# An adaLN transformer block on one core: the rows of w_mod dealt to the partitions in neighbouring fives, the conditioning vector loaded in that form, and the order of all instructions replaced

## The chip, the cores and the metric

The kernel runs on one core of a Trainium2 chip. The time is device microseconds of one execution, lower is better; a time given for a kernel is the median of its runs. One further execution is recorded by the hardware profiler, and all rows of the profile come from that one.

## The reference

```
mod = (silu(c) @ w_mod).reshape(1, 6, 1, 640)      # c: 1 x 640, w_mod: 640 x 3840
sa, ca, ga, sb, cb, gb = the six rows of mod
h = layernorm(x) * (1 + ca) + sa                    # x: 1 x 2048 x 640, bf16
q, k, v = split(h @ wqkv)                           # 32 heads of 20
p = softmax(where(0 <= i - j < 256, q k^T / sqrt(20), -1e9))
x = x + ga * ((p v) @ wo)
h = layernorm(x) * (1 + cb) + sb
x = x + gb * ((sigmoid(h @ w_gate) * (h @ w_up)) @ w_down)    # 640 -> 1536 -> 640
```

Only c and w_mod are touched in their layout. Whatever the order, out[f] = sum over the 640 rows d of silu(c)[d] · w_mod[d, f], so the rows may be dealt to the 128 partitions in any way as long as c is dealt in the same way.

## The kernel before, in words

The 2,048 rows are worked in chunks of 256. For a chunk, x is normalised (ln_stats on DVE and POOL), transposed to hT (columns on partitions, five tiles of 128), modulated with 1 + ca and sa, and projected with wqkv. The products q and k are laid out per head as QT and KT, by TensorE transpositions through PSUM in the first chunks (matmuls M from ident and stg) and later by DMA transpositions. The scores of four heads at a time are written to the PSUM tile S (L693), ACT takes their exp into E (L1019), POOL or DVE cuts out the window (L1044), TensorE multiplies E with V (bursts of matmuls M from E and V), DVE transposes the sums (L1088) and normalises into On, and SP stores On to a scratch array doc in HBM and loads it back as oT, transposed. Then come the output projection with wo (L1149 adds it to x), the second layer norm, and the feed-forward with the weights wg, wu and wd (sigmoid on ACT L1194, product on DVE L1196, result added at L1215). The score sets are interleaved with all other matmuls. For every chunk but the first there are, for each half of the heads, four main sets and one edge's set, which takes the blocks at both ends of the window; its score matmuls are 128x64.

At the start, silu of c is made in small steps and spread to a tile silubc; the modulation sums are matmuls of silubc with w_mod. w_mod comes in three parts of 1,280 columns, loaded into memory that later holds wd, wu and hh, so the profile calls them wd, wu and hh from in_w_mod_dram. wqkv comes in slices of columns (four of 320, then one of 640), all through SP's DMA queue in the order in which SP issues them. The gate ga is brought to HBM as `gate`, loaded to all partitions as gbc, and multiplied into wo on DVE (L1238), five times 128x640. Until real work is there, TensorE runs matmuls on zeros (L672, L682).

What sets the order is a table of numbers. `build()` records every operation in program order; the n-th recorded operation takes the n-th entry of PRIO. The entry modulo 5 names the engine (pe, act, dve, pool, sp), and the operations are issued on each engine in the order of their entries. The same walk hands out the buffers of each pool. `emit()` then writes the semaphore waits which the data and the buffers need, and makes POOL wait for DVE operations that hold the shared port ahead of it in the table.

```
        o.prio = PRIO[self.seq] if PRIO else prio
        for o in sorted(self.ops, key=lambda x: x.prio):
            e = ENGS[o.prio % 5]
```

c is loaded by ACT's queue in five rows of 128 numbers into a corner of the buffer of oT (c_row), transposed by one matmul with ident into PSUM (tile psc, 128x5) and halved by DVE into c_col, from which tanh and silu follow. Partition p so holds the numbers p, 128 + p, 256 + p, 384 + p and 512 + p of c, and the same five rows of w_mod.

Of the kernel before, what the change touches and what calls it, by code (L numbers as in the profile page):

```python
# [8 lines left out]
ALU = mybir.AluOpType  # L9
# [8 lines left out]
NDT = D // 128  # L18
# [343 lines left out]
def c_pe(n):  # L362
# [148 lines left out]
def build(nc, A_x, A_wqkv, A_wo, B_x, B_w_gate, B_w_up, B_w_down, c, w_mod, out, S=2048):  # L511
    NCH = S // CH
    P = Prog(nc)
    A = P.op
# [3 lines left out]
    def sb(name, shape, dtype=BF16):  # L518
        return nc.alloc_sbuf_tensor(name, shape, dtype)
# [9 lines left out]
    ident = sb("ident", [128, 128])  # L529
# [761 lines left out]
```

## Time and profile before

| | |
|---|---|
| median of 3 runs | 323.55 us (323.23 to 323.64) |
| profiled execution, its own time | 324.34 us |
| span of the profiled execution | 322.6 us |
| granted TensorE clock, mean | 1.000 |
| TensorE matmuls | 316.8 us busy, 4,877 |
| TensorE weight loads | 223.2 us, 4,877 |
| VectorE (DVE) | 207.1 us, 420 |
| ScalarE (ACT) | 218.0 us, 327 |
| GpSimd (POOL) | 177.0 us, 268 |
| HBM read, written | 21.30 MB, 5.25 MB |

The profile gives times from the span's start; "[0.80 <-DMA wqkv<-in_A_wqkv_dram]" behind a row is the idle time of that engine ahead of the row and what ended it. SPq and ACTq are the issues of DMAs on SP and ACT, not the transfers. A row with "x10" holds ten instructions of one shape one after the other, with the time from the start of the first to the end of the last.

### The profile page before, as it was taken

How to read it: one execution, taken by the hardware profiler on the slowest of the kernel's cores; microseconds unless marked ns; L12 is line 12 of the kernel's file. 1: busy time of each engine (PE TensorE's matmuls, PEld its weight loads, DVE VectorE, ACT ScalarE, POOL GpSimd, SP SyncE). 2: the span in 40 equal slices, each digit the busy share in tenths (PEclk: the TensorE clock that was granted, in tenths of full speed). 3: DMA queues.
4: the chain of work that ended last, by engine and by line, in shares of the span. 5: the costliest groups of instructions: out<-in, count | busy, mean ns of one | idle time of the engine just before them, and what ended most of it. 6: DMA issues, size and time to landing. Idle time of an engine off the chain costs nothing.

```text
span 322.6 us, 11622 instructions
## 1 busy us (share of the span) xinstructions
PE 316.8 (98%) x4877; PEld 223.2 (69%) x4877; DVE 207.1 (64%) x420; ACT 218.0 (68%) x327; POOL 177.0 (55%) x268
## 2 busy tenths in 40 slices
PE   8899999999999999999999999999999999999996
PEld 3565545556876577767766667876887788887885
DVE  5688997886689658683756565637572765464232
ACT  2689888799887979688878686877767563110120
POOL 4237985978566675856566555666547366002000
PEclk9999999999999999999999999999999999999999
DMA  7979999799992753465024572530222031305101
GB/s 229 364 246 394 233 214 177 146 171 207 274 156 48 118 93 87 99 95 144 9 63 93 94 111 69 71 93 13 68 65 67 2 83 34 90 3 63 42 22 41
DMA packets 71182, 37.85 MB, mean 117 GB/s; under 512 B 45274, under 2 KB 69338, under 8 KB 71130
## 3 DMA queue, kind: packets, MB, share of 16 engines
q1 hardware_dynamic: 70112, 35.96, 50.2%
q10 hardware_dynamic: 1018, 1.15, 1.1%
q8 instruction: 38, 0.62, 0.8%
q14 instruction: 14, 0.11, 0.1%
HBM read 21.30 MB, written 5.25 MB: 82 GB/s over the span
## 4 chain that ended last, share of the span: by engine, by line
PE 92%; SPq 3%; DMA 2%; issue 1%; ACT 1%; DVE 0%; ACTq 0%
PE M L692 76%; PE S L693 8%; PE M L693 7%; SPq L588 3%; DMA wqkv<-in_A_wqkv_dram 2%; ACT E L1019 1%; DVE hh L1196 0%; ACT sig L1194 0%; DVE x L1215 0%; ACTq L335 0%
## 5 line engine op out<-in xcount | busy, mean ns | idle before, releaser
L1019 ACT ACTIVATE E<-S 128x512 bf16<-128x512 f32 (+2 forms) x184 | 150.4, 878 | 38.1 <-PE S L693 34.9
L1044 POOL TENSOR_SCALAR_AFFINE_SELECT E<-E 128x512 bf16<-128x512 bf16 (+1 forms) x176 | 139.3, 819 | 58.1 <-ACT E L1019 18.8
L692 PE MATMUL M<-wqkv,hT 128*128 128x480 bf16 (+1 forms) x340 | 73.0, 355 | 1.6 <-DMA wqkv<-in_A_wqkv_dram 1.6
L692 PE MATMUL M<-h2T,wu 128*128 128x256 bf16 x480 | 64.8, 273 | 0.0
L692 PE MATMUL M<-h2T,wg 128*128 128x256 bf16 x480 | 64.6, 273 | 0.0
L1196 DVE SCALAR_TENSOR_TENSOR hh<-sig,M 128x512 bf16<-128x512 f32 x48 | 32.5, 682 | 42.1 <-ACT sig L1194 28.4
L692 PE MATMUL M<-wd,hh 128*128 128x320 bf16 (+2 forms) x396 | 57.7, 295 | 0.1
L1194 ACT ACTIVATE sig<-M 128x512 f32<-128x512 f32 x48 | 28.9, 601 | 39.5 <-PE M L692 37.7
L692 PEld LDWEIGHTS M<-h2T,wg 128*128 128x128 bf16 x480 | 45.8, 98 | 8.1 <-issue 0.2
L692 PEld LDWEIGHTS M<-h2T,wu 128*128 128x128 bf16 x480 | 45.7, 98 | 7.5
L692 PEld LDWEIGHTS M<-wqkv,hT 128*128 128x128 bf16 x340 | 30.5, 98 | 28.0 <-DMA wqkv<-in_A_wqkv_dram 1.9
L692 PEld LDWEIGHTS M<-wd,hh 128*128 128x128 bf16 x396 | 37.4, 98 | 14.7 <-DVE hh L1196 0.3
L693 PEld LDWEIGHTS S<-QT,KT 20*64 20x64 bf16 (+1 forms) x1856 | 19.9, 100 | 19.4 <-ACT E L1019 8.1
L693 PE MATMUL S<-QT,KT 20*64 20x256 bf16 (+5 forms) x1856 | 32.1, 228 | 0.2 <-ACT E L1019 0.2
L1215 DVE TENSOR_TENSOR x<-M,x 128x320 bf16<-128x320 f32 (+2 forms) x33 | 15.7, 475 | 25.3 <-PE M L692 25.1
L778 DVE BATCH_NORM_STATS2 st<-x 128x6 f32<-128x320 bf16 x64 | 28.2, 477 | 2.2 <-DMA x<-in_A_x_dram 1.9
L1088 DVE STREAM_TRANSPOSE T<-M 128x512 f32<-128x512 f32 x32 | 21.6, 698 | 9.7 <-PE M L693 9.4
L692 PE MATMUL M<-wo,oT 128*128 128x320 bf16 x160 | 25.9, 300 | 0.1
L784 POOL TENSOR_SCALAR st<-st 128x2 f32<-128x2 f32 (+1 forms) x17 | 4.0, 235 | 37.0 <-DVE st L780 34.9
L693 PE MATMUL M<-E,V 128*32 128x128 bf16 (+1 forms) x960 | 22.8, 246 | 0.0
L693 PEld LDWEIGHTS M<-E,V 128*32 128x32 bf16 x960 | 19.0, 97 | 4.1 <-POOL E L1044 1.9
L1149 DVE TENSOR_TENSOR x<-M,x 128x320 bf16<-128x320 f32 x32 | 15.3, 482 | 8.9 <-PE M L692 8.6
(78 smaller groups left out, 237.1 us busy)
## 6 DMA issues: line engine op xcount, KB each, us to landing
x<-in_A_x_dram SPq DMA_DIRECT2D x23, 160.0 KB
doc<-On SPq DMA_DIRECT2D x64, 40.0 KB
wd<-in_B_w_down_dram SPq DMA_DIRECT2D x4, 480.0 KB
out_dram<-x SPq DMA_DIRECT2D x11, 160.0 KB
wqkv<-in_A_wqkv_dram SPq DMA_DIRECT2D x4, 400.0 KB
wu<-in_w_mod_dram SPq DMA_DIRECT2D x5, 320.0 KB
oT<-doc SPq DMA_DIRECT2D x8, 192.0 KB
wd<-in_w_mod_dram SPq DMA_DIRECT2D x4, 320.0 KB
```

Source lines behind the costliest of these rows:

```text
L588: return e.dma_start(dst(), src())
L692: return e.matmul(o, l, r, start=st, stop=sp, skip_group_check=True)
L693: return e.matmul(o, l, r, start=st, stop=sp, tile_position=tp, skip_group_check=True)
L778: A("dve", lambda e, g, bi=bi, j=j: e.bn_stats(v(bi * 12 + j * 6, 6), src[bi].ap[:, j * 320:(j + 1) * 320]), 0.48, reads=[src[bi].r()], wr ...
L784: A("pool", lambda e, g, lo=lo, hi=hi: e.tensor_scalar(v(28 + lo, hi - lo), var()[:, lo:hi], EPS, None, op0=ALU.add), 0.2, reads=[st.r(("m ...
L1019: A("act", lambda e, eng: e.activation(dst(), src(), ACT.Exp, scale=SM_SCALE), c_act(n), reads=[Sp.r()], writes=[E.r(key)], prio=3, tag=f" ...
L1044: A("pool", lambda e, eng: e.affine_select(rows(dst), rows(src), pattern=[[0, 8], [sign, n]], compare_op=ALU.is_ge, fill=0.0, base=base, c ...
L1088: A("dve", lambda e, g, h=h: e.transpose(T1.ap[:, 512 * h:512 * h + 512], X[h].ap), 0.694, reads=[X[h].r()], writes=[T1.r(h)], prio=3.5, t ...
L1149: A("dve", lambda e, g, ps=ps, bi=bi, half=half: e.tensor_tensor(x1[bi].ap[:, half * 320:half * 320 + 320], ps.ap[:, 0:320], x1[bi].ap[:, ...
L1194: A("act", lambda e, g, pg=pg, sg=sg: e.activation(sg.ap[:], pg.ap[:], ACT.Tanh, scale=0.5), c_act(512), reads=[pg.r()], writes=[sg.r()], ...
L1196: A("dve", lambda e, g, pu=pu, sg=sg, f0=f0: e.scalar_tensor_tensor(out=hh.ap[:, f0:f0 + 2, :], in0=sg.ap[:].rearrange("p (a b) -> p a b", ...
L1215: A("dve", lambda e, g, ps=ps, bi=bi, c0=c0, n=n: e.tensor_tensor(x1[bi].ap[:, c0:c0 + n], ps.ap[:, 0:n], x1[bi].ap[:, c0:c0 + n], op=ALU. ...
```

## The change

Three things are changed. The five rows of w_mod that a partition holds are neighbours, 5p to 5p + 4, in place of rows 128 apart. c is loaded straight into a tile of its own, c_in, with the same five numbers on each partition (128 pieces of 10 B in place of five of 256 B), and the transposing matmul and its PSUM tile are gone. And every entry of PRIO is another, so that all engines issue in a new order, with some operations on other engines than before. Line numbers after this place are smaller by 3 in the new kernel.

```
 PRIO = [
-    118, 123, 218, 113, 73, 693, 288, 513, 1493, 93, 503, 67, 258, 332, 302, 743, 126, 4, 29, 39, 44, 49, 54, 59, 34,
...
-    c_row = p_oT.aps[0][0:NDT, 0, 0:128]
+    c_in = sb("c_in", [128, NDT])
...
-    dma(lambda: c_row, lambda: c.rearrange("o (t p) -> (o t) p", p=128), 0.05, writes=[R_crow], prio=-1, eng="act")
-    wm_src = w_mod.rearrange("(t p) f -> p t f", p=128)
+    dma(lambda: c_in[:], lambda: c.rearrange("o (p t) -> (o p) t", t=NDT), 0.1, writes=[R_crow], prio=-1, eng="act")
+    wm_src = w_mod.rearrange("(p t) f -> p t f", t=NDT)
...
-    psc = Tile(p_M, "psc")
-    p_oT.init[0].append(A("pe", lambda e, g: e.matmul(psc.ap[:, 0:NDT], c_row, ident[0:NDT, 0:NDT], start=True, stop=True), 0.1,
-      reads=[R_crow, R_ident], writes=[psc.r()], prio=0, lat=0.2, tag="ctr", ni=2))
-    A("dve", lambda e, g: e.tensor_scalar(c_col[:], psc.ap[:, 0:NDT], 0.5, None, op0=ALU.mult), 0.17, reads=[psc.r()], writes=[R_ccol], prio=0)
+    A("dve", lambda e, g: e.tensor_scalar(c_col[:], c_in[:], 0.5, None, op0=ALU.mult), 0.17, reads=[R_crow], writes=[R_ccol], prio=0)
```

SP's order near the start, where it issues the slices of wqkv and the loads of x, before:

```order
8 L588 DMA wqkv<-in_A_wqkv_dram 128x5x320
9 L588 DMA wqkv<-in_A_wqkv_dram 128x5x640
10 L588 DMA x<-in_A_x_dram 128x640
11 L588 DMA wqkv<-in_A_wqkv_dram 128x5x320
12 L588 DMA x<-in_A_x_dram 128x640
```

and after:

```order
8 L588 DMA wqkv<-in_A_wqkv_dram 128x5x320
9 L588 DMA wqkv<-in_A_wqkv_dram 128x5x640
10 L588 DMA wqkv<-in_A_wqkv_dram 128x5x320
11 L588 DMA x<-in_A_x_dram 128x640
12 L588 DMA wu<-in_w_mod_dram 128x1280 x2
```

The last 320-column slice of wqkv is issued ahead of the next load of x, not behind it.

TensorE's order at the first edge's score set, before (S from QT and KT are score sets, M from wqkv and hT projections):

```order
76 L693 MATMUL S<-QT,KT 128x64 x32
77 L692 MATMUL M<-wqkv,hT 128x480 x5
78 L692 MATMUL M<-ident,stg 128x128 x8
79 L692 MATMUL M<-wqkv,hT 128x480 x2
80 L693 MATMUL S<-QT,KT 64x256 x8
```

and after:

```order
75 L690 MATMUL S<-QT,KT 128x64 x32
76 L689 MATMUL M<-ident,stg 128x128 x8
77 L689 MATMUL M<-wqkv,hT 128x480 x10
78 L690 MATMUL S<-QT,KT 64x256 x8
```

Ten projection matmuls stand between the edge's set and the next, not seven.

SP's order where the gate is loaded to all partitions (gbc), before:

```order
33 L806 DMA_TRANSPOSE KT<-stg 128x8x128
34 L806 DMA_TRANSPOSE QT<-stg 128x8x128
35 L588 DMA gbc<-gate 128x640
36 L588 DMA doc<-On 20x4x256
37 L588 DMA oT<-doc 128x2x256
38 L588 DMA doc<-On 20x4x256 x3
```

and after:

```order
31 L803 DMA_TRANSPOSE KT<-stg 128x8x128
32 L803 DMA_TRANSPOSE QT<-stg 128x8x128
33 L588 DMA doc<-On 20x4x256 x4
34 L588 DMA gbc<-gate 128x640
35 L803 DMA_TRANSPOSE KT<-stg 128x8x128
```

The load of gbc stands behind four stores of attention results, not ahead of them.

DVE's order where wo is scaled with gbc, before:

```order
71 L1238 TENSOR_TENSOR wo<-wo,gbc 128x640 x3
72 L909 CAST stg<-M 128x24x20
73 L1088 STREAM_TRANSPOSE T<-M 128x512
74 L1238 TENSOR_TENSOR wo<-wo,gbc 128x640 x2
75 L778 BN_STATS st<-x 128x6 x2
76 L780 BN_AGGR st<-st 128x2
77 L909 CAST V<-M 128x24x20
```

and after:

```order
70 L906 CAST stg<-M 128x24x20
71 L1235 TENSOR_TENSOR wo<-wo,gbc 128x640 x4
72 L739 TENSOR_SCALAR scB<-T 128x5
73 L1235 TENSOR_TENSOR wo<-wo,gbc 128x640
74 L906 CAST V<-M 128x24x20
75 L775 BN_STATS st<-x 128x6
76 L1085 STREAM_TRANSPOSE T<-M 128x512 x2
```

All five scalings stand ahead of the cast of V and both transpositions T, where three stood ahead of them before and the transpositions came between.

223 rows, old and new, of the table PRIO are left out of this document.

## The prediction

> **What bounds the kernel now.** The page's busy line comes first, then, from its part on the chain that ended last, the shares by engine.
>
> ```profile
> PE 316.8 (98%) x4877; PEld 223.2 (69%) x4877; DVE 207.1 (64%) x420; ACT 218.0 (68%) x327; POOL 177.0 (55%) x268
> PE 92%; SPq 3%; DMA 2%; issue 1%; ACT 1%; DVE 0%; ACTq 0%
> ```
>
> TensorE works for 98% of the span and carries 92% of the chain. An average hides stages, so the busy time by stretch comes next (start and end, length, then each engine's busy time in the order PE, weight loads, DVE, ACT, POOL, then granted clock, DMA share and GB/s).
>
> ```profile
> 0.00:11.00 11.00, 8.87 (x82) 4.42 (x82) 4.92 (x18) 3.76 (x8) 3.94 (x21) 1.00 0.83 260
> 11.00:19.30 8.30, 7.50 (x76) 4.55 (x76) 7.51 (x21) 6.85 (x13) 2.74 (x10) 1.00 0.90 307
> 19.30:60.00 40.70, 40.47 (x649) 22.88 (x650) 34.80 (x77) 35.72 (x58) 30.51 (x45) 1.00 1.00 246
> 60.00:272.00 212.00, 211.80 (x3663) 151.92 (x3661) 138.03 (x267) 163.86 (x238) 136.66 (x187) 1.00 0.48 96
> 272.00:320.20 48.20, 48.18 (x414) 39.48 (x411) 21.53 (x41) 7.78 (x13) 3.11 (x6) 1.00 0.19 41
> 320.20:322.60 2.40, 0.00 (x0) 0.00 (x0) 0.29 (x1) 0.00 (x0) 0.00 (x0) 1.00 0.20 59
> ```
>
> From 19.30 to 320.20 TensorE is busy for 40.47 + 211.80 + 48.18 = 300.45 of 300.90 us, at full clock. Only 0.45 us is idle there. What an order can change lies before 19.30, in those gaps, in the 2.40 us after the last matmul, or in what the matmuls themselves take. Matmul ends are modelled, so a row's own length says less than the step from one start to the next.
>
> The chain shows what ends last ahead of 19.30.
>
> ```profile
> 11.25 8.00 DMA wqkv<-in_A_wqkv_dram
> 19.30 1.87 PE M L692 x16
> 42.17 1.58 ACT E L1019 x3
> 43.80 0.43 PE S L693 x24
> ```
>
> Two things besides TensorE stand on these steps. The last 320-column slice of wqkv is issued at 11.25, lands 8.00 us later and releases a projection. At 43.80 a score set waits for the exp of the set before it to free its banks. The timeline rows give the same places with their idle time in brackets.
>
> ```profile
> 10.97 2.40 PE L692 MATMUL M<-wqkv,hT 128*128 128x320 bf16 x15 [0.81 <-DMA wqkv<-in_A_wqkv_dram]
> 10.14 1.07 SPq L588 DMA_DIRECT2D x<-in_A_x_dram  x1
> 11.25 0.43 SPq L588 DMA_DIRECT2D wqkv<-in_A_wqkv_dram  x1
> 19.30 1.53 PE L692 MATMUL M<-wqkv,hT 128*128 128x320 bf16 x10 [0.80 <-DMA wqkv<-in_A_wqkv_dram]
> 43.80 0.43 PE L693 MATMUL S<-QT,KT 20*64 20x256 bf16 x24 [0.23 <-ACT E L1019]
> ```
>
> **The change part by part.**
>
> *The matmuls.* One matmul of 5 columns goes (4876 against 4877). I counted tile-shape changes along both orders: 170 in each, with the same matmuls of each shape. If every pair of neighbouring shapes costs what its starts are apart in the trace, the two orders differ by under 0.1 us. I take 0.
>
> *The conditioning vector.*
>
> ```profile
> 0.79 0.56 ACTq L588 DMA_DIRECT2D oT<-in_c_dram  x1
> 3.98 0.18 PE L657 MATMUL M<-ident,oT 5*128 5x5 bf16 x1
> 4.20 0.17 DVE L659 TENSOR_SCALAR c_col<-M 128x5 bf16<-128x5 f32 x1
> 4.84 0.47 ACT L663 ACTIVATE silubc<-siluc 128x320 bf16<-128x320 bf16 x1 [0.23 <-DVE siluc L661]
> 4.09 2.12 PE L672 MATMUL S<-E 128*128 128x512 bf16 x6
> 6.18 0.46 PE L692 MATMUL S<-silubc,wd 128*128 128x64 bf16 x10
> 8.93 0.35 PEld L692 LDWEIGHTS S<-silubc,wd 128*128 128x128 bf16 x10 [0.35 <-DMA wd<-in_w_mod_dram]
> 10.19 0.17 DVE L764 COPY mA<-S 128x10 f32<-128x10 f32 x1 [2.12 <-PE S L692]
> ```
>
> The transposition takes 0.18 us at 3.98, between warming matmuls on zeros that last until 6.18. silubc, the end of the small chain, is ready at 4.84 + 0.47 = 5.31, so 0.87 us of cover lies between it and its first user, and later users wait for w_mod (the 0.35 at 8.93). Removing the step is worth 0. The load now comes in 128 pieces of 10 B, not five of 256 B. Nothing shows such a load; the nearest row is the load as it was, read at most 3.98 − 0.79 = 3.19 us after its issue, and half as long again would be 1.6 us, 0.7 more than the cover. Also, c_col is now DVE's first work but one, and the statistics of x stand behind it. Both end in hT, ahead of which DVE stands idle for 2.12 us, until the sums over w_mod are there. That hides the 0.7. Bounds 0 and, with a load three times as slow, 6.4 − 0.87 − 2.12 = +3.4; I take 0, by the nearest row.
>
> *The dealing of w_mod.* Each partition still reads pieces of 2,560 or 1,280 B, with the same bytes in the same order in SP's queue. Only the step from one partition's piece to the next grows from 7,680 to 38,400 B. No trace of before has that step, so the bounds go both ways: nearest are the same loads themselves, which with the other loads ran at 260 GB/s in the first 11 us. I take 0, and price a slowing as a rival.
>
> The Trainium skill ("DMA: Bandwidth & Descriptors", section "Latency and other measured facts") speaks against changed row steps in one case: copies whose row pitch in HBM is a large power of two slow down, from 207 GB/s at 512 KiB to 103 at 4 MiB, by a cause that it calls an inference. 38,400 B is no such pitch, so whoever follows the page to the letter gives rival C below no chance and the term 0; by the page's worst ratio of rates the 4.4 us of C would double. No run so far shows either.
>
> *Term 1, the last 320-column slice of wqkv.* SP now issues it ahead of a 160 KB load of x, not behind it.
>
> ```profile
> 12.00:16.00 4.00, 4.00 (x44) 2.63 (x44) 3.24 (x10) 3.32 (x8) 1.66 (x7) 1.00 1.09 375
> 16.00:20.00 4.00, 3.20 (x34) 1.98 (x33) 3.27 (x8) 3.88 (x5) 1.08 (x3) 1.00 0.61 200
> ```
>
> The queue is drained at 375 GB/s while it is full, so the slice lands 163,840 B / 375 GB/s = 0.44 us earlier. The issue itself is 11.25 − 10.14 = 1.11 us earlier, but the queue and not the issue sets the landing, since it takes 8.00 us. Bounds: 0, if the last of the 16 engines to finish is held by something else (the drop to 200 GB/s before 19.30 says that some engines had run dry while the load was unfinished), and the whole visible wait, 0.80. I take −0.45.
>
> *Term 2, the slice issued second.* The first two slices of wqkv (issued together) land as before, but the new order reaches the second slice's weights after six matmuls of the first slice on the new rows of hT, not after eight. Ten such matmuls take 1.53 us (the row at 19.30), so this is 2 × 0.15 = 0.30 us earlier for a load that lands when it did. The modulations ahead of them are dealt otherwise too: four of a run on DVE, then three on POOL, where DVE had six and POOL one.
>
> ```profile
> 10.46 1.43 DVE L848 TENSOR_SCALAR hT<-hT,mA 128x128 bf16<-128x128 bf16 x6
> 12.34 0.45 POOL L848 TENSOR_SCALAR hT<-hT,mA 128x128 bf16<-128x128 bf16 x1 [4.96 <-DVE hT L838]
> ```
>
> One takes 1.43 / 6 = 0.24 us on DVE and 0.45 on POOL. Part of the 0.30 is waiting that is there already. Bounds 0 and +0.40 (the 0.30, and half of what a POOL modulation takes longer); I take +0.20.
>
> *Term 3, the score set at 43.80.* Between the first edge's set (128x64) and the next set stood 5 + 2 projection matmuls and 8 transposing ones; now ten projections and the same eight.
>
> ```profile
> 41.19 0.41 PE L693 MATMUL S<-QT,KT 20*128 20x64 bf16 x32
> 41.53 1.19 PE L692 MATMUL M<-wqkv,hT 128*128 128x480 bf16 x5
> 42.56 0.61 PE L692 MATMUL M<-ident,stg 128*128 128x128 bf16 x8
> 43.00 0.57 PE L692 MATMUL M<-wqkv,hT 128*128 128x480 bf16 x2
> ```
>
> Three more projections at 1.19 / 5 = 0.24 us are some 0.7 us of cover against a wait of 0.23. It goes whole: bounds −0.30 (the wait with its change of shape) and 0 (exp later as well); I take −0.25. Behind it exp is some 0.4 us early.
>
> *Term 4, the end.* The last wide store is now issued just before the last narrow one. The 2.40 us after 320.20 hold 0.29 us of DVE and the last store; a second transfer beside it costs 0 to +0.20. I take +0.05.
>
> *Sum.* −0.45 + 0.20 − 0.25 + 0.05 = −0.45 us. The profiled execution took 324.34 us (span 322.6 and 1.74 around it), so 323.89 against it; it was 0.79 above the median of the three runs, 323.55. The forecast for a median is 323.10 us. About 0.2% (0.65 us) is what a measurement of this kernel can tell from no change. The forecast's own bounds, 0 to −0.80, 0 to +0.40, 0 to −0.30, 0 to +0.20 and one small unseen wait, give 322.4 to 324.1.
>
> **The rivals.**
>
> *A: the first waits go whole (faster).* If that slice of wqkv was late only because the x load lay ahead of it on the engine that finished last, all of the 0.80 at 19.30 goes, and the 0.25 at 43.80 with it, and an order that spaces the rest better also removes a late one like this:
>
> ```profile
> 214.29 0.93 PEld L692 LDWEIGHTS M<-wd,hh 128*128 128x128 bf16 x8 [0.29 <-DVE hh L1196]
> ```
>
> That is −0.80 − 0.25 − 0.29 = −1.34, without term 2: 322.2 us. For it: the slice is the longest wait of the chain. Against: bytes ahead of it explain only 0.44.
>
> *B: the gate's broadcast comes too late and DVE's queue stands (slower).* Before, SP issued gbc right behind QT; now four doc stores stand ahead of it.
>
> ```profile
> 43.45 1.78 SPq L806 DMA_TRANSPOSE QT<-stg  x1
> 45.31 0.53 SPq L588 DMA_DIRECT2D gbc<-gate  x1
> 46.88 1.16 SPq L588 DMA_DIRECT2D doc<-On  x3
> 50.70 1.49 DVE L1238 TENSOR_TENSOR wo<-wo,gbc 128x640 bf16<-128x640 bf16 x3
> 56.70 0.61 DVE L909 CAST V<-M 128x480 bf16<-128x480 f32 x1
> 54.99 2.20 PE L692 MATMUL M<-wqkv,hT 128*128 128x480 bf16 x10
> ```
>
> Four stores at 1.16 / 3 = 0.39 us put the issue at about 46.9, or 48.1 if the last waits for its On as it did. Before, the scaling began 50.70 − 45.31 = 5.39 us after the issue, which bounds the landing from above: so 52.3 to 53.5 now at the latest. On DVE all five scalings (1.49 / 3 = 0.50 us each) now stand ahead of the cast of V with one small step, for which I take 0.4, where three stood before, and the transpositions of T came between. Behind the waiting scaling are queued that cast and both T transpositions, and the projection at 54.99 needs the bank that the cast frees. The cast would end at 52.3 + 2.5 + 0.4 + 0.6 = 55.8 to 57.0: a wait of 0.8 to 2.0, say 1.4, and 324.5 us. It decides from a landing about 51.5, some 4.6 us after the issue. For it: the doubled queue. Against: DVE was only free at 50.70, so the true landing may be far earlier.
>
> *C: w_mod lands slower.* Its first 1,600 KB stand ahead of wqkv in the queue; at 375 GB/s they take 4.4 us, and a fifth more puts 0.9 us on the first projection: 324.0 us. This is also the rival that the new form is no gain but a cost.
>
> **How the numbers follow.** Forecast 0.50, A 0.18, B 0.22, C 0.10. The time is the forecast's, 323.1. The range 321.7 to 324.9 holds A, C and B's middle, and leaves some 0.2 to the ends of A and B. Faster (under 322.9): A's 0.18 and 0.18 of the forecast, 0.36. Slower (over 324.2): 0.20 of B, 0.08 of C where the slowing is larger than a fifth, 0.08 of the forecast where term 2 and an unseen wait add up, 0.36. Same: 0.28.
>
> **What would show each step.** The wait of the projection on wqkv shrinks from 0.80 to some 0.35 (forecast), goes (A) or stays. The bracket with exp at the set after the edge's set is gone. The five wo scalings show a wait for gbc, and the projection behind the cast of V a wait for DVE, if B holds. The first projection starts near 10.97 unless C holds. From there to the last matmul TensorE needs 309 us less those waits, whatever the order; were it longer with no wait in brackets, the claim that the order's work is equal would be wrong, and the prediction with it.

## The result, and the profile after

The changed kernel took 325.10 us (median of 5, 324.81 to 325.28) against 323.64 for the kernel before (median of 5, 323.23 to 324.20): a ratio of 1.0042, with an interval of 1.0031 to 1.0054. It is slower, where 323.1 was forecast with a range of 321.7 to 324.9. In two later jobs, with twelve runs of the changed kernel beside 35 of before, the ratio was 1.0022 (1.0004 to 1.0039) and 1.0011 (0.9991 to 1.0031). The changed kernel came out above before in all three, but in the third the interval holds 1; the size did not hold.

The two profiled executions differ less than the first medians: 324.81 (span 323.1) against 324.34 (span 322.6), since that of before was its slowest of six and that of after its fastest of five. A second profile of before is shown with the experiments.

The busy line and the shares of the chain, after:

```profile
PE 316.8 (98%) x4876; PEld 223.6 (69%) x4876; DVE 213.2 (66%) x434; ACT 212.5 (66%) x314; POOL 174.4 (54%) x267
PE 95%; DMA 2%; DVE 1%; issue 1%; SPq 1%; ACT 0%; DVEq 0%; ACTq 0%
```

TensorE works exactly as long as before (316.8 us), and from the start of the first projection to the end of the last matmul it needs 309.0 us against 309.2, so the claim that the order's work is equal held. The difference lies in when it starts and where it stands still. The chain of work that ended last, after, in order of time (start, length, what):

```profile
2.64 5.83 DMA wd<-in_w_mod_dram
8.52 0.47 PE S L689 x10
...
10.31 0.71 PE S L689 x22
11.31 0.33 DVE hT L845
11.78 0.44 PE M L689 x2
...
41.17 0.23 PE S L690 x9
41.39 0.51 issue
41.91 0.35 PE S L690 x23
```

Before, it ran through SP and the last 320-column slice of wqkv to 19.30. That wait is gone. It now runs through a slice of w_mod, and through a stretch of 0.51 us at 41.39 in which TensorE waits for nothing that the profile shows. The timeline rows of after at these places, with the idle time ahead of a row and what ended it in brackets:

```profile
8.52 0.47 PE L689 MATMUL S<-silubc,wd 128*128 128x64 bf16 x10 [1.24 <-DMA wd<-in_w_mod_dram]
10.26 0.75 PE L689 MATMUL S<-silubc,wd 128*128 128x64 bf16 x20
11.78 2.39 PE L689 MATMUL M<-wqkv,hT 128*128 128x320 bf16 x14 [0.77 <-DVE hT L845]
19.33 1.52 PE L689 MATMUL M<-wqkv,hT 128*128 128x320 bf16 x10
41.91 0.35 PE L690 MATMUL S<-QT,KT 20*128 20x64 bf16 x23 [0.51 <-issue]
42.65 2.19 PE L689 MATMUL M<-wqkv,hT 128*128 128x480 bf16 x10
44.76 0.42 PE L690 MATMUL S<-QT,KT 20*64 20x256 bf16 x23
287.50 0.99 PEld L689 LDWEIGHTS M<-h2T,wg 128*128 128x128 bf16 x10 [0.39 <-DVE x L1146]
```

The first projection starts at 11.78 and not at 10.97, and waits for the modulated hT, no longer for wqkv. The projection of the late slice (19.33) and the score set behind the first edge's set (44.76) have lost their brackets, as forecast. New are the bracket in the middle of the edge's set, after nine of its 32 matmuls, and one at 287.50, where a bank comes free late because two statistics stand on DVE between the additions.

Counted from start to start of neighbouring matmuls against their usual step, this is the account between the two profiled executions: start of the first projection +0.81, from there to the first score set +0.09, late slice −0.87, score set behind the edge's set −0.30, the edge's set +0.70, the wait at 287 +0.27, two small waits of before near 92 and 214 that are gone −0.24, many small steps together +0.15, behind the last matmul about −0.1. Together about +0.5, which is the difference of the spans.

The start is the least certain part of it. Two later profiles of the changed kernel (a_again and a_ctl, below) start the first projection at 11.88 and 11.33, one of before (b_again) at 11.20. And an earlier start is not yet time: a_ctl starts 0.45 us ahead of after and its span is 323.0 against 323.1.

### The profile page after: what moved, and what is told of

It is laid out like the page before. It is cut to its first block, busy times and chain, and to the rows that moved or that the text cites. A ratio compares the mean times of both kernels' runs of the same rounds, so it can differ in the third digit from the quotient of the medians.

```text
span 323.1 us, 11632 instructions
## 1 busy us (share of the span) xinstructions
PE 316.8 (98%) x4876; PEld 223.6 (69%) x4876; DVE 213.2 (66%) x434; ACT 212.5 (66%) x314; POOL 174.4 (54%) x267
## 4 chain that ended last, share of the span: by engine, by line
PE 95%; DMA 2%; DVE 1%; issue 1%; SPq 1%; ACT 0%; DVEq 0%; ACTq 0%
PE M L689 79%; PE S L690 8%; PE M L690 7%; DMA wd<-in_w_mod_dram 2%; SPq L588 1%; PE S L689 0%; DVE x L1146 0%; PE S L679 0%; ACT hT L869 0%; DVE st L775 0%; DVE hT L845 0%; DVE x L1212 0%; DVE mA L761 0%; DVEq L335 0%; ACT V L905 0%
## 5 line engine op out<-in xcount | busy, mean ns | idle before, releaser
L689 PE MATMUL M<-h2T,wg 128*128 128x256 bf16 x480 | 63.2, 273 | 0.1
L689 PE MATMUL M<-h2T,wu 128*128 128x256 bf16 x480 | 63.0, 273 | 0.0
L689 PE MATMUL M<-wd,hh 128*128 128x320 bf16 (+2 forms) x396 | 56.8, 295 | 0.0
L689 PE MATMUL M<-wo,oT 128*128 128x320 bf16 x160 | 24.9, 299 | 0.0
L906 DVE CAST stg<-M 128x480 bf16<-128x480 f32 (+1 forms) x31 | 17.8, 576 | 9.5 <-PE M L689 9.5
```

What stands on the lines that cost most here:

```text
L689: return e.matmul(o, l, r, start=st, stop=sp, skip_group_check=True)
L906: return e.tensor_copy(dst(), src())
```

## The experiments

Each kernel was run with the kernel before on the same chip. Medians and, because executions scatter by 0.5 us and more, the mean less the mean of before in the same job (a_best2 and b_form each without one execution far off, 328.84 and 329.06; their medians have it):

| kernel | runs | median | mean less before's | ratio (interval) |
|---|---|---|---|---|
| b_again | 12 | 323.97 | −0.33 | 0.9995 (0.9978 to 1.0011) |
| b_deal | 12 | 324.24 | −0.26 | 0.9997 (0.9981 to 1.0013) |
| a_deal | 12 | 324.93 | +0.47 | 1.0018 (1.0003 to 1.0033) |
| a_loads | 12 | 324.49 | +0.03 | 1.0003 (0.9985 to 1.0022) |
| a_again | 12 | 324.99 | +0.71 | 1.0022 (1.0004 to 1.0039) |
| a_fetch | 12 | 325.67 | +1.52 | 1.0044 (1.0024 to 1.0063) |
| b_slice | 12 | 323.80 | −0.27 | 0.9995 (0.9976 to 1.0015) |
| a_best | 12 | 325.27 | +1.03 | 1.0031 (1.0013 to 1.0048) |
| a_fetch2 | 5 | 325.01 | +0.83 | 1.0032 (1.0020 to 1.0044) |
| a_best2 | 12 | 325.04 | +0.99 | 1.0034 (1.0013 to 1.0055) |
| b_form | 12 | 324.75 | +0.64 | 1.0022 (1.0004 to 1.0041) |
| a_ctl | 12 | 324.73 | +0.46 | 1.0011 (0.9991 to 1.0031) |
| a_hh | 12 | 325.02 | +0.54 | 1.0018 (0.9994 to 1.0043) |
| a_hh_loads | 12 | 324.85 | +0.46 | 1.0013 (0.9991 to 1.0036) |
| a_hh_loads_old | 12 | 323.77 | −0.21 | 0.9997 (0.9979 to 1.0015) |
| a_gbc | 12 | 325.03 | +1.51 | 1.0046 (1.0025 to 1.0067) |
| a_mend | 12 | 324.39 | +0.55 | 1.0014 (1.0000 to 1.0029) |
| a_mend_t | 12 | 324.48 | +0.69 | 1.0018 (1.0004 to 1.0033) |

The kernel before, run once more as b_again, came out 0.33 beside itself, and the changed kernel at +0.71 and +0.46 in two jobs: differences of 0.3 in this column say nothing.

**The kernel before again: is its late slice always there?** No edit.

> The kernel before once more, unchanged, for a second profile of it. Its profiled execution (span 322.6, time 324.34) lay 0.7 us above the median of five runs (323.64). Theory 'late slice': what varies between executions is how late the last 320-column slice of wqkv lands, so a usual execution has less than 0.8 us of waiting before the projection that stood at 19.30, and a span near 321.9. Theory 'spread everywhere': the wait is 0.8 us again and the span is near 322.6 or lower for other reasons. Time ratio 1.000 within 0.002.

The row of b_again that answers to the one at 19.30:

```profile
18.70 1.52 PE L692 MATMUL M<-wqkv,hT 128*128 128x320 bf16 x10
```

No bracket: the slice was in time, and the span is 322.1. In b_deal (the next experiment), which has the same order, the wait was there again:

```profile
19.84 1.40 PE L692 MATMUL M<-wqkv,hT 128*128 128x320 bf16 x9 [0.87 <-DMA wqkv<-in_A_wqkv_dram]
```

Of the four profiles with before's place for this slice, two have the wait (before, b_deal) and two have not (b_again, b_form below). So what term 1 removes is a wait of some executions, and the median holds only a part of it.

**The dealing alone, put into before and taken out of after.**

```
b_deal   -    wm_src = w_mod.rearrange("(t p) f -> p t f", p=128)
         +    wm_src = w_mod.rearrange("(p t) f -> p t f", t=NDT)
a_deal   -    wm_src = w_mod.rearrange("(p t) f -> p t f", t=NDT)
         +    wm_src = w_mod.rearrange("(t p) f -> p t f", p=128)
```

In both, c keeps its own dealing, so silu(c) meets other rows: the sums are other numbers, the work is the same.

> The kernel before with only the dealing of w_mod's rows changed to neighbouring fives (c is left as it was, so each number of silu(c) meets another row: the sums are other numbers, the work is the same). Theory 'dealing': the larger row step makes some DMA engines late, the slices of w_mod and the first of wqkv land 0.3 to 0.4 us later, the first projection starts near 11.35 and not 10.97, and the time is 0.3 to 0.5 us longer. Theory 'small pieces of c': the loads are late because of the 128 pieces of c, so nothing changes here: 10.97 and 0.0 us. Theory 'order': the same, 0.0 us.

> The changed kernel with the old dealing of w_mod's rows, c still loaded in neighbouring fives (so silu(c) meets other rows: the sums are other numbers, the work is the same). Theory 'dealing': w_mod lands 0.3 to 0.4 us earlier, the first projection starts near 11.4 and not 11.78, and the time is 0.3 to 0.5 us below the changed kernel's 325.1. Theory 'small pieces of c': no change, 11.78 and 325.1. Theory 'order': most of it stays, 325.0.

At first this looked like the cause: the first projection started at 11.40 in b_deal and at 11.24 in a_deal. The times did not follow (−0.26 and +0.47, as b_again and the changed kernel), and later runs with the new dealing started at 11.23 (a_hh) and even at 10.70:

```profile
10.70 1.97 PE L689 MATMUL M<-wqkv,hT 128*128 128x320 bf16 x11 [0.81 <-DMA wqkv<-in_A_wqkv_dram]
```

That is a_hh_loads, earlier than any run with the old dealing. Counted over the packet records of the traces, a packet of 2,560 B of w_mod in the first 12 us took 102 ns in the median with either dealing, and 125 to 134 ns in the mean with the old one (before, b_again, b_slice, a_deal) against 126 to 139 with the new (11 kernels). In the three kernels with the old dealing and c in 640 pieces (below) the mean is 110 to 119, and no run tells these two apart. As a cost of its own the dealing fell. What scatters, with either, is how late the last part of a load lands. In the traces each load reports its landing in 16 parts, and the first slice of wqkv was complete at 11.30, 11.44 and 10.90 in three profiles of the changed kernel, and at 10.92 and 10.97 in two of before.

**The order of w_mod's slices.** The new order swaps the second slice with the third, and the halves of the fifth. In the listing of SP all read "wd<-in_w_mod_dram 128x1280", so it can't be seen there.

```
 PRIO (entries 18 to 23: the loads of w_mod's first part)
-    29, 44, 39, 49, 59, 54
+    29, 39, 44, 49, 54, 59
```

> The changed kernel with the slices of w_mod issued in the order of before (second slice ahead of the third, and the two halves of the fifth swapped back); nothing else. Theory 'order': the second group of modulation sums no longer waits 1.24 us for its slice at 8.52, the sums end near 10.4 and not 11.04, and the first projection then waits for wqkv alone and starts near 11.35: 0.4 us below the changed kernel, 324.7. Theory 'dealing' alone: the slices land as late as they did and the first projection stays near 11.78, 325.1.

The rows of a_loads that answer to 8.52 and 11.78 of after:

```profile
8.12 0.46 PE L689 MATMUL S<-silubc,wd 128*128 128x64 bf16 x10
11.37 0.88 PE L689 MATMUL M<-wqkv,hT 128*128 128x320 bf16 x4 [0.78 <-DVE hT L845]
```

The row at 8.12 is the same second group of sums: the wait of 1.24 is gone, and the first projection starts 0.41 us earlier, as the theory had it. One pair of profiles would not show it, since the changed kernel itself once started at 11.33 (a_ctl). Over all profiles with the new order, the new dealing and the swapped slices it started at 11.78, 11.88, 11.59, 11.37, 11.33, 11.23 and 11.76 (mean 11.56), with the slices in the old order at 11.37, 10.70, 11.28 and 11.10 (mean 11.11). Counted from the landing of the first slice of wqkv, which takes the scatter of the loads out, the start came 0.41 to 0.54 us later in the eight profiles with swapped slices (a_deal among them) and 0.04 to 0.29 later in those four. So of the 0.81 some 0.4 is the swap (0.47 against 0.05 in before), and 0.38 is a later landing (11.30 against 10.92). In time a_loads stood 0.03 over before where a_again, in another job, stood 0.71 over it; the same edit gave nothing in a_hh_loads below.

**The slice of term 1, put into before.**

```
 PRIO (before: entries 26, a slice of wqkv, and 241, a load of x)
-    264, ... 209
+    209, ... 264
```

> The kernel before with one change, the last 320-column slice of wqkv issued ahead of two loads of x (the one term of the change that was forecast as a gain). Theory 'late in some executions': the slice waits 0.96 us in some executions of before and 0.09 in others, so here it is always 0.09, the profile shows no bracket with wqkv at the first projection of that slice, and the mean is 0.3 to 0.5 us below before with a smaller spread. Theory 'hidden anyway': mean the same within 0.15.

No bracket with wqkv is left at that projection, and from the first projection to the end of the last matmul it took 308.1 us, the least of all profiles (309.2 and 308.5 for before). The mean is 0.27 lower, but b_again was 0.33 lower with no edit at all, so the gain in time is not shown.

**The changed kernel again, and the stall in the edge's set.** a_again has no edit; a_fetch moves two loads on SP.

```
 PRIO (after: entries 39, the last load into hh, and 64, a load of wg)
-    1304, ... 1359
+    1639, ... 1644
```

> The changed kernel once more, unchanged, beside the others on one chip and for a second profile. Theory 'three places' (first projection late by dealing and order, a new stall of TensorE inside the first edge's set, a new wait at 287): first projection near 11.7, 0.5 to 0.7 us of idle time inside the edge's set near 41, 0.27 near 287, and a time 0.4 to 1.2 us over the kernel before. Theory 'one bad execution': the stall at 41 is not there again.

> The changed kernel with two loads (640 KB of w_mod into hh, 384 KB of wg) issued on SP behind the loads of x, three stores and the load of wu, not ahead of them; nothing else. Theory 'late instructions': TensorE stops inside the edge's set at 41.4 because the 16 KB of its own instructions, which came at 39.44 in place of 38.15, had to wait behind these loads; with them moved the fetch starts near 38 and the stall of 0.5 to 0.7 us goes: 0.5 us below a_again. Theory 'late transposition': the stall is a wait for QT or KT, whose transpositions come no earlier, and it stays.

In a_again the first projection (11.88), the stall (0.51) and the wait at 287 all stood as in the first profile. The next lines are of the DMA queues: the row of TensorE's instruction fetch (count, MB, share) in before from 38 to 40 us, in after from 39 to 41, and in a_fetch from 36 to 39.

```profile
q8 instruction: 1, 0.02, 3.0%
q8 instruction: 1, 0.02, 3.6%
q8 instruction: 1, 0.02, 2.4%
```

After has none from 36 to 39. The 16 KB come about 1.3 us later than before, behind 640 KB for hh; with these moved they come ahead of 39 again, and the edge's set of a_fetch runs through, 32 matmuls without a bracket:

```profile
40.95 0.41 PE L690 MATMUL S<-QT,KT 20*128 20x64 bf16 x32
48.94 2.19 PE L689 MATMUL M<-wqkv,hT 128*128 128x480 bf16 x10 [1.32 <-ACT E L1016]
54.27 2.07 DVE L1235 TENSOR_TENSOR wo<-wo,gbc 128x640 bf16<-128x640 bf16 x4 [0.98 <-DMA gbc<-gate]
57.50 1.19 PE L689 MATMUL M<-wqkv,hT 128*128 128x480 bf16 x5 [0.59 <-DVE V L906]
59.29 0.99 PE L689 MATMUL M<-wo,oT 128*128 128x320 bf16 x6 [0.61 <-DMA oT<-doc]
```

So the stall is TensorE's own instructions arriving late, and not a transposition. The other traces bear it out: in the six profiles that stall there the fetch began between 38.61 and 39.53, in the 14 that do not by 38.22. And the stall ends 1.3 to 1.5 us behind the end of the 16 KB packet each time (in after the packet ran from 39.44 to 40.60, and TensorE went on at 41.91). The time is 0.8 longer all the same: the loads now stand right ahead of KT's transposition, and waits of 1.32, 0.59 and 0.61 us took the place of 0.51. (The row at 48.94 names ACT; KT's buffer is the other thing that it waits for, and in a_hh the same row names it.) The rows from 54.27 to 57.50 are rival B: DVE waits for gbc, the cast of V stands behind, and TensorE waits for that cast. The profiled execution is a late one, 326.75 against a median of 325.67, so these waits may be longer than usual; so it is with a_best, 326.40 against 325.27.

**All mended at once, and the loads moved further.** a_best adds to a_fetch the old dealing (c to match, in 640 pieces), the old order of the slices, and DVE's additions near 286 ahead of both statistics. a_fetch2 moves the loads elsewhere, and a_best2 is a_best with those places.

```
 PRIO (after)      entry 39 (hh)   64 (wg)   224 (wu)   2025, 2026 (statistics)
 after                  1304        1359      1634        9837, 9842
 a_best                 1639        1644      1634        9892, 9897
 a_fetch2               1589        1899      2144        9837, 9842
 a_best2                1589        1899      2144        9892, 9897
```

> The changed kernel with four things mended: w_mod dealt as before (c loaded to match, 640 pieces of one number), w_mod's slices issued in the order of before, the two loads of a_fetch moved back, and DVE's four additions near 286 ahead of the four statistics. Theory 'three places': first projection near 11.0, no stall in the edge's set, no wait at 287, so 0.3 + 0.4 + 0.6 + 0.25 = 1.5 us below a_again, and 0.2 to 0.6 below before. If the 640 pieces of c land too late, the first projection moves beyond 11.3 and shows it.

> The changed kernel with three loads moved on SP: 640 KB of w_mod into hh behind the loads of x and three stores, 384 KB of wg behind the load of gbc, 576 KB of wu behind the transpositions of hT near 58. In a_fetch the loads stood right ahead of the transposition of KT, which landed at 48.80 in place of 46.06 and made TensorE wait 1.3 us. Theory 'late instructions': here TensorE's instructions are fetched near 37 to 38, the stall in the first edge's set (0.70) is gone, KT lands before 46 and no wait takes the stall's place: 0.5 to 0.7 us below the changed kernel. Theory 'the bytes must go somewhere': a wait of the same size turns up at a later transposition or at oT, near 57 to 66.

> a_fetch2 with three more mends: w_mod dealt as before (c loaded to match, in 640 pieces of one number), w_mod's slices issued in the order of before, DVE's four additions near 286 ahead of the four statistics. In a_best the first projection started at 11.01 and the wait at 287 was gone. Theory 'three places': first projection near 11.0, idle time behind it 2.4 us in place of 3.37, a span near 321.5: 1.4 us below the changed kernel and 0.5 to 0.8 below before. Theory 'the bytes must go somewhere': no better than before.

a_best started at 11.01 and had a_fetch's waits (1.39, 0.95, 0.37). a_fetch2 had none of these but one of 0.91 at 76.14, ahead of a score set. a_best2 came without them, and stopped at a later fetch, again 1.35 us behind the end of its packet (52.08 to 53.04):

```profile
54.39 0.97 PE L689 MATMUL M<-wqkv,hT 128*128 128x480 bf16 x4 [0.59 <-issue]
```

None reached its expected time. In both best kernels the wait at 287 went and one of 0.22 or 0.23 for hh came at 292 or 294.

**The first half of the change alone, in the old order.** b_form: the diff above without the table, and the old table without the entry of the transposition.

> The kernel before with the first half of the change complete (w_mod in neighbouring fives, c loaded in that form, no transposition) and its own old order with that one matmul taken out. Theory 'dealing': the first slice of wqkv lands near 11.25 as in b_deal and the first projection starts 0.2 to 0.4 us later; 0 to 0.4 us over before. Theory 'small pieces of c': more than in b_deal, 0.4 us and up. Theory 'only the order counts': 0.0.

The first projection started at 11.24, so nothing beyond b_deal. The time is 0.9 longer in the median, and 0.6 in the mean without the execution at 329.1; another lies at 327.0. The profiled one was the 327.0; its large waits are for late DMAs:

```profile
37.69 0.86 PE L690 MATMUL M<-wu,silubc 128*32 128x320 bf16 x20 [1.08 <-DMA wu<-in_w_mod_dram]
50.96 1.17 PE L689 MATMUL M<-wqkv,hT 128*128 128x480 bf16 x5 [2.07 <-DMA KT<-stg]
```

Before has neither. Since b_deal showed no such thing and c's pieces are long in by then, I can't name a mechanism by which the form would do this; it stays open whether the new form costs something.

**The stair on one chip.** a_ctl is the changed kernel; a_hh moves one load; each next kernel adds one mend.

```
 PRIO (after)     39 (hh)     19, 20, 22, 23 (w_mod)     dealing
 a_ctl             1304         44, 39, 59, 54             new
 a_hh              1589         44, 39, 59, 54             new
 a_hh_loads        1589         39, 44, 54, 59             new
 a_hh_loads_old    1589         39, 44, 54, 59             old, c in 640 pieces
```

> The changed kernel unchanged, as the first step of a stair on one chip: 0.7 us or more over before; first projection near 11.7 to 11.9, 0.7 us of stall in the first edge's set, 0.27 at 287.

> The changed kernel with one DMA moved: the 640 KB load of w_mod into hh is issued on SP behind the two loads of x and three stores, not ahead of wg. All else keeps its place, so the bytes ahead of KT's transposition are the same. Theory 'late instructions': the fetch of TensorE's instructions starts near 38.5 in place of 39.5, the stall in the edge's set falls from 0.70 to 0.1 or 0.2, KT lands as before, and the time is 0.5 us below a_ctl. Theory 'the bytes must go somewhere': the stall goes and an equal wait turns up.

> a_hh with w_mod's slices issued in the order of before as well. Theory 'order': first projection near 11.35 in place of 11.8, a further 0.4 us below a_hh. Theory 'hidden anyway': the same as a_hh.

> a_hh_loads with w_mod dealt as before (c loaded to match, in 640 pieces of one number). Theory 'dealing': first projection near 11.0, a further 0.3 us below a_hh_loads and in all 1.2 us below a_ctl, 0.3 to 0.5 below before. Theory 'the dealing costs nothing': the same as a_hh_loads.

The stall went in a_hh with this one load (in a_ctl it was 0.49), and the start came forward in a_hh_loads to 10.70 (11.23 in a_hh, 11.33 in a_ctl). The time gained nothing: +0.46, +0.54, +0.46. Rows of a_hh (three) and of a_hh_loads (three) show what came instead:

```profile
47.66 1.17 PE L689 MATMUL M<-wqkv,hT 128*128 128x480 bf16 x5 [0.40 <-DMA KT<-stg]
53.05 2.07 DVE L1235 TENSOR_TENSOR wo<-wo,gbc 128x640 bf16<-128x640 bf16 x4 [1.03 <-DMA gbc<-gate]
56.27 1.19 PE L689 MATMUL M<-wqkv,hT 128*128 128x480 bf16 x5 [0.64 <-DVE V L906]
```

```profile
52.18 2.07 DVE L1235 TENSOR_TENSOR wo<-wo,gbc 128x640 bf16<-128x640 bf16 x4 [1.07 <-DMA gbc<-gate]
55.40 1.19 PE L689 MATMUL M<-wqkv,hT 128*128 128x480 bf16 x5 [0.68 <-DVE V L906]
57.21 1.53 PE L689 MATMUL M<-wo,oT 128*128 128x320 bf16 x10 [0.62 <-DMA oT<-doc]
```

When TensorE arrives earlier, gbc has not, and the time is given back at 55 to 57. In the changed kernel itself DVE began these scalings at 52.73 with no bracket. a_hh_loads_old was the only one of these kernels without a wait between 40 and 80 and came out with before (0.9997). It started at 11.36, later than a_hh_loads and against the forecast of 11.0, so the old dealing did not help by an early start. Its c in 640 pieces makes silubc 1.4 us later (its step on ACT begins at 6.14, in a_hh_loads at 4.74). In the three kernels with such a c the 16 parts of the first slice of wqkv land within 0.8 to 0.9 us of each other, in all others within 1.2 to 1.8. Whether that is why its later loads come in time is open.

**The floor under it.** gbc ahead of the four stores, alone; then with the mends of a_hh_loads; then with one of the two statistics moved.

```
 PRIO (after)     39     19, 20, 22, 23      221 (gbc)    2026
 a_gbc           1304    44, 39, 59, 54       1714        9842
 a_mend          1589    39, 44, 54, 59       1714        9842
 a_mend_t        1589    39, 44, 54, 59       1714        9892
```

> The changed kernel with one DMA moved: gbc is loaded ahead of the four stores to doc, as before, not behind them. In a_hh and a_hh_loads, where TensorE came to the place 0.5 to 1.2 us earlier, DVE waited 1.03 and 1.07 us for gbc and TensorE 0.64 and 0.68 us for V behind it; in the changed kernel itself DVE never waited there. Theory 'floor': the late gbc is a floor that the changed kernel does not reach, because its late start and its stall already hold TensorE back, so here the time stays that of the changed kernel, within 0.3 us. Theory 'gbc costs by itself': 0.5 us less.

> a_hh_loads with gbc moved as in a_gbc: new dealing, slices of w_mod in the old order, the load into hh behind the stores, gbc ahead of them. Theory 'floor': first projection near 11.1, no stall in the edge's set, no wait of DVE for gbc nor of TensorE for V near 55, at most 0.3 for oT; idle time behind the first projection near 2.8 us in place of 4.5, span near 321.9: 0.7 to 1.0 us below a_hh_loads and 0.2 to 0.6 below before. Theory 'the bytes must go somewhere': a wait of 0.5 us or more turns up between 45 and 76 and the time is no better than before.

> a_mend with one of DVE's statistics near 286 moved behind the two additions that free TensorE's banks. The wait of 0.27 near 287 goes; in a_best, where two were moved, 0.38 appeared at 291.6 in its place. If only the total of DVE's work counts there, the wait moves again and nothing is gained; if the order counts, 0.2 us below a_mend.

a_gbc gained nothing, so no cost of gbc's place in the changed kernel by itself is to be seen. a_mend was 0.64 below a_gbc in the median and 0.95 in the mean on the same chip, and no wait for gbc or V was left, but waits for KT and oT were:

```profile
47.53 2.19 PE L689 MATMUL M<-wqkv,hT 128*128 128x480 bf16 x10 [0.22 <-DMA KT<-stg]
57.10 1.53 PE L689 MATMUL M<-wo,oT 128*128 128x320 bf16 x10 [0.48 <-DMA oT<-doc]
```

But two executions of a_gbc lie at 327.0 and 327.8. Against before, where 0.2 to 0.6 less was expected, a_mend stays 0.55 over, no better than a_hh_loads beside its own before (0.46). So the floor of gbc is there, and mending it did not bring the time down. In a_mend_t the wait at 287 turned into 0.27 for hh at 292.30: in this profile DVE's total counts there, not its order. No version beat the kernel before beyond the scatter.

## Why the prediction was wrong, point by point

- **The same bytes in the same order in SP's queue** failed. It was read from shapes that are alike. The slices were swapped, the group of sums that needs the second waited 1.24 us for a landing at 8.47, and the first projection was 0.81 us late in the profile. Some 0.4 of it is the swap, by a_loads, by the means over the profiles (0.45) and by the count from wqkv's landing; the rest is a later landing, which moved by 0.54 between three profiles of the changed kernel.
- **One small unseen wait** in the bounds of the sum, which left it about nothing, was too small: the stall of 0.51 us (0.70 against the usual step; 0.34 to 0.51 in the six profiles of kernels with these loads in this place) is TensorE's instructions, fetched behind the 640 KB that the new order issues at that point. The page of before has the queue (q8), and no term of the sum spoke of it. The Trainium skill ("Runtime: NRT & Kernel Launch", section "Instruction fetch mechanics") says that instructions are refilled in blocks of 16 KiB by a DMA queue of their own and that crossing a block is mostly hidden. The size agrees with the trace, one packet of 16,384 B. Of the 38 such packets of the changed kernel this one was not hidden, with a busy queue in front.
- **Term 1** was right in its place: −0.45 was forecast, and −0.87 came between the two profiles. The wait is in some executions of before only, so the forecast took one execution for all; what it is worth in the mean no run shows, since b_slice's −0.27 is no more than b_again's −0.33.
- **Term 2** had the sign and not the mechanism: +0.20 was forecast, mostly for reaching the second slice of wqkv sooner (POOL's slower modulation stood in its bounds with 0.1), and the stretch from the first projection to the first score set grew by 0.09. Its two late steps wait for modulated rows of hT from ACT and from POOL, not for a load, as the weight loads of after show:

```profile
12.19 1.35 PEld L689 LDWEIGHTS M<-wqkv,hT 128*128 128x128 bf16 x11 [0.19 <-ACT hT L844]
13.85 0.25 PEld L689 LDWEIGHTS M<-wqkv,hT 128*128 128x128 bf16 x3 [0.31 <-POOL hT L845]
```

- **Term 3** held: −0.25 forecast, −0.30 found. But with "Behind it exp is some 0.4 us early" it looked past the edge's set, where the stall came. **Term 4** was +0.05 and came as about −0.1. The zero for **the conditioning vector** held: silubc began at 4.78, before at 4.84.
- **Rival A** had its waits right: the one at 19.30 went whole, and those at 43.80 and 214.29 went too. Its 322.2 still missed by 2.9, since it had nothing for the three places either. **Rival B** has its mechanism as told, DVE for gbc and TensorE for V, at a price of 0.59 to 0.95 in four profiles and not 1.4, but not in the changed kernel: the scaling there began without a wait. It shows only where TensorE comes earlier. **Rival C** fell with the packet times and the start at 10.70.

The four terms came to about −0.87 + 0.09 − 0.30 − 0.1 = −1.2 between the two profiles, and to about −0.3 against an execution of before without the late slice. What made the sign was outside them: +0.81, +0.70 and +0.27, at three places where the prediction had 0. The cause of each of these waits is shown, but for the 0.38 of later landing in the first. That they add up to the slower time is an account of two profiles only: the kernels in which they were mended got other waits, and but for a_loads and a_hh_loads_old none came back to the time of before.

## What to carry to other kernels

When a whole order is replaced, rows that read alike still hide swaps: follow each load to its user by number, above all among the slices that the first work waits for. Where one engine is busy all the time and long transfers are queued, ask where its own instructions are fetched, and how much stands ahead of each fetch. Before a wait is counted as a gain, look at a second execution for whether it is there, and at what is late next: here two places were mended in a_hh_loads, other waits came at 55 to 57, and the time stayed.

## What the runs showed of the hardware

TensorE can run dry in the middle of a set of matmuls because of its instruction fetch: 0.51 us up to 41.91 in after, 0.59 up to 54.39 in a_best2, each ending 1.3 to 1.4 us behind the end of the 16 KB packet. And the same loads in the same order land apart from one execution to the next: the first projection of the changed kernel started at 11.78, 11.88 and 11.33.
